# Attention with V as the stationary operand, row sums on VectorE, one-tile FFN passes and DMA transposes, on one core

## The chip, the cores and the metric

The kernel runs on one core of one Trainium2 chip. The metric is the device time of one execution in microseconds (us), and less is better. TensorE does the matmuls, ScalarE (ACT) the exps and tanhs, VectorE (DVE) the elementwise work, GpSimd (POOL) a few small steps of the layer norms, and SyncE (SP) issues every DMA on one queue. Quoted times are medians of several executions. All runs below were timed beside the kernel before on the same chip.

## The reference, cut to what matters

The layer works on 2048 tokens of width 1024: attention with 32 query heads of 32 that share one K and one V head, then a gated FFN of width 3584. Inputs are bf16.

```python
q = (layernorm(x) @ wq)                     # 32 heads x 32; k, v: one head x 32
p = softmax(q @ k.T * 32 ** -0.5)           # 32 x 2048 x 2048 scores
h = x + (p @ v) @ wo
g, u = layernorm(h) @ w_gate, layernorm(h) @ w_up
out = h + (sigmoid(g) * u) @ w_down
```

There are 134 million scores, so 1024 exps of 128 x 1024 each (the profile of the kernel before lists them as 128x1024 x1024, 1052 ns on average), and neither kernel avoids any of them. The rest is matmuls, which TensorE has to run while ScalarE works through the exps.

## The kernel before

Both kernels are written as a plan: a small list scheduler at build time orders the instructions of all engines (`pl.op(engine, function, dependencies, ...)`), and that fixed order is emitted with semaphores. While attention runs, the scheduler puts a visit to the scores (`emit_S`) on TensorE whenever ScalarE is about to run dry, and fills the time between with other groups of matmuls. `Pr` holds exponentiated scores with keys on the partitions. `sigmoid(g)*u` is computed as `0.5*(tanh(g/2)+1)*u`.

A score visit covers 128 queries of 4 heads and 4 key tiles. It has 4 rounds of 4 row-tiled matmuls, because a head of 32 fills only a quarter of the array's rows (the profile lists these matmuls as 32*128 and plain ones as 128*128). Each of the four has its own quarter, and they run side by side: by the median they start 4 ns apart, and the rounds follow each other at about 56 ns, as single plain matmuls of 128 columns do:

```python
for kk in range(KB):                       # KB = 4 key tiles
    for j in range(4):                     # 4 heads, one on each quarter of the rows
        last = pl.op("pe", mm(S_ps[:, bank, kk * P:(kk + 1) * P], kT4[DH * j:DH * (j + 1), kt * P:(kt + 1) * P],
                              QTb[DH * j:DH * (j + 1), c % 2, g, qo:qo + P], True, True, tile_position=(DH * j, 0)), ...)
for i in range(2):                         # two exps, 1024 wide
    exps[u] = pl.op("act", lambda: ACT.activation(out=Pr[:, slot, :]..., in_=S_ps[:, pb:pb + 2, :], func=ACTF.Exp, scale=SCALE), ...)
```

In P V the exponentiated scores are the stationary operand (128 x 128, loaded for each matmul: 8192 loads in the profile for 8192 matmuls), and V with a column of ones moves through (33 columns). The row sum arrives as column 33, so DVE only takes a reciprocal and multiplies. The result has tokens on its partitions, so TensorE transposes it before the output projection:

```python
for j in range(4):
    for kt in range(NT):                   # 16 key tiles
        ... mm(F_ps[:, b, j * VS:j * VS + DH + 1], Pr[:, slot, co:co + P], Vaug[:, kt, 0:DH + 1], kt == 0, kt == NT - 1)
... DVE.reciprocal(rL...); DVE.tensor_tensor(Osb = ov * rL); PE.transpose(Osb -> OT)
```

The FFN works in 8 chunks of 256 tokens. Its gate and up weights stream from HBM once for every chunk, in transfers of 512 KB through a ring:

```python
for w in range(2):                         # gate, up: 256 tokens move
    for dt in range(DT):
        ... mm(F_ps[:, b, w * 256:(w + 1) * 256], wgu[:, sl, w, dt, fo:fo + P], hnT[:, dt, :], dt == 0, dt == DT - 1)
```

The softmax here doesn't subtract the row's maximum and nothing guards it: scores larger than these inputs give would overflow.

## Time and profile before

The first timing gave 1219.02 us (1218.07 to 1223.41, 3 runs). The profiled execution took 1223.8 us.

| | before |
|---|---|
| TensorE busy, 60 to 1060 us | 975.6 of 1000 us |
| ScalarE busy, 60 to 1060 us | 975.4 of 1000 us |
| after the last exp (1060.6 us to the end) | 163 us, almost only FFN matmuls |
| matmuls of P V | 8192, one about every 25 ns |

Here are the page's busy time of each engine (with its share of the span and count of instructions) and its busy tenths in 40 slices of the span:

```profile
PE 1174.0 (96%) x22016; PEld 835.1 (68%) x22016; DVE 316.4 (26%) x838; ACT 1042.1 (85%) x1283; POOL 47.2 (4%) x109
...
PE   4899979999999999999999999999999999999999
...
ACT  6899999999999999999999999999999989711120
```

The last five digits of the ACT row are the tail, in which ScalarE has almost nothing left and TensorE is still full. These are the page's chain of waits by engine, and two of its groups (busy us, mean ns of one, idle time before):

```profile
PE 63%; ACT 31%; issue 3%; DVE 2%; POOL 0%; DMA 0%
...
L495 ACT ACTIVATE Pr<-S_ps 128x1024 bf16<-128x1024 f32 x1024 | 972.4, 1052 | 26.4 <-PE S_ps L330 25.9
...
L330 PE MATMUL F_ps<-Vaug,Pr 128*128 128x33 bf16 x8192 | 244.4, 178 | 2.4 <-issue 1.5
```

The view by windows has, for each stretch, its length and then the busy time of PE, PEld, DVE, ACT and POOL (with counts), the granted TensorE clock, the busy share of the DMA engines and GB/s:

```profile
60.00:1060.00 1000.00, 975.59 (x20038) 686.54 (x20036) 239.31 (x635) 975.40 (x1171) 20.15 (x45) 0.99 0.39 111
...
1060.00:1224.00 164.00, 159.59 (x1283) 117.21 (x1279) 35.97 (x80) 23.14 (x58) 1.34 (x3) 1.00 0.63 163
```

Two engines are full at once for 1000 us. This is how TensorE's time looks in the timeline (start us, length us, and matmuls in a run):

```profile
502.98 0.40 PE L330 MATMUL S_ps<-QTb,kT 32*128 32x128 bf16 x16
503.31 1.52 PE L330 MATMUL F_ps<-Vaug,Pr 128*128 128x33 bf16 x54
504.68 0.27 PE L330 MATMUL F_ps<-hnT,ring 128*128 128x256 bf16 x1
504.88 0.40 PE L330 MATMUL S_ps<-QTb,kT 32*128 32x128 bf16 x16
```

A run of 54 P V matmuls takes 1.52 us with its last latency included.

### The profile page before, as it was taken

The page shows a single profiled execution, that of the slowest core. Times are in us where ns is not written, and L with a number is a line of the kernel's source. Part 1 is how long each engine was busy: PE and PEld are TensorE (multiplying, and loading weights), DVE is VectorE, ACT ScalarE, POOL GpSimd, SP SyncE. Part 2 cuts the span into 40 slices and gives each one's busy share as a digit, 9 for nine tenths or more (in the row PEclk, how much of TensorE's full clock was granted, in tenths as well). Part 3 has the DMA queues.
Part 4 walks back from the last instruction along what each step waited for, and adds up shares of the span by engine and source line. Part 5 has one row for each costly group of instructions (what it writes and reads, how often), then busy time and mean ns, then how long its engine had stood idle before and what let it go on. Part 6 is the DMA issues. An engine that isn't in the chain of part 4 may idle for free.

```text
span 1223.8 us, 47137 instructions
## 1 busy us (share of the span) xinstructions
PE 1174.0 (96%) x22016; PEld 835.1 (68%) x22016; DVE 316.4 (26%) x838; ACT 1042.1 (85%) x1283; POOL 47.2 (4%) x109
## 2 busy tenths in 40 slices
PE   4899979999999999999999999999999999999999
PEld 3665557785678756877568675778657776587684
DVE  8523321212222222223121222132222212232121
ACT  6899999999999999999999999999999989711120
POOL 6100000000000000000000000000000000000000
PEclk9999989999999999999999999999999999999999
DMA  9411175562056601565016460256303653089390
GB/s 320 116 28 41 42 260 156 148 173 64 20 149 174 192 20 46 150 191 148 16 50 191 119 170 20 70 165 184 111 20 86 172 148 102 15 224 263 105 252 18
DMA packets 258612, 151.02 MB, mean 123 GB/s; under 512 B 7280, under 2 KB 248944, under 8 KB 258416
## 3 DMA queue, kind: packets, MB, share of 16 engines
q1 hardware_dynamic: 258416, 148.00, 43.1%
q8 instruction: 173, 2.83, 1.0%
q14 instruction: 23, 0.19, 0.0%
HBM read 140.64 MB, written 7.34 MB: 121 GB/s over the span
## 4 chain that ended last, share of the span: by engine, by line
PE 63%; ACT 31%; issue 3%; DVE 2%; POOL 0%; DMA 0%
PE F_ps L330 54%; ACT Pr L495 28%; PE S_ps L330 9%; ACT tnh L669 1%; ACT zone L313 1%; PE F_ps L619 0%; ACT zone L230 0%; DVE OT L566 0%; DVE st L274 0%; DVE st L276 0%; PE F_ps L558 0%; DMA ring<-in_A_x_dram 0%; POOL dsb L287 0%; DVE hnT L625 0%; DVE ring L307 0%
## 5 line engine op out<-in xcount | busy, mean ns | idle before, releaser
L495 ACT ACTIVATE Pr<-S_ps 128x1024 bf16<-128x1024 f32 x1024 | 972.4, 1052 | 26.4 <-PE S_ps L330 25.9
L330 PE MATMUL F_ps<-hnT,ring 128*128 128x256 bf16 x3584 | 440.6, 275 | 2.5 <-DVE OT L566 1.2
L330 PEld LDWEIGHTS F_ps<-hnT,ring 128*128 128x128 bf16 x3584 | 332.5, 98 | 61.3 <-issue 3.1
L330 PEld LDWEIGHTS F_ps<-Vaug,Pr 128*128 128x128 bf16 x8192 | 229.7, 96 | 28.1 <-issue 4.1
L330 PE MATMUL F_ps<-Vaug,Pr 128*128 128x33 bf16 x8192 | 244.4, 178 | 2.4 <-issue 1.5
L330 PE MATMUL S_ps<-QTb,kT 32*128 32x128 bf16 x8192 | 208.5, 218 | 15.4 <-ACT Pr L495 10.1
L330 PE MATMUL F_ps<-zone,hact 128*128 128x512 bf16 x896 | 213.2, 380 | 0.8 <-DVE OT L566 0.5
L330 PEld LDWEIGHTS S_ps<-QTb,kT 32*128 32x128 bf16 x8192 | 119.2, 93 | 127.9 <-ACT Pr L495 81.6
L676 DVE SCALAR_TENSOR_TENSOR hact<-tnh,F_ps 128x256 bf16<-128x256 f32 x224 | 94.3, 421 | 384.0 <-ACT tnh L669 383.9
L669 ACT ACTIVATE tnh<-F_ps 128x256 f32<-128x256 f32 x224 | 90.7, 405 | 115.0 <-PE F_ps L330 115.0
L330 PEld LDWEIGHTS F_ps<-zone,hact 128*128 128x128 bf16 x896 | 79.2, 98 | 91.3 <-DVE OT L566 0.7
L330 PE MATMUL F_ps<-zone 128*128 128x256 bf16 (+2 forms) x512 | 76.5, 292 | 3.1 <-POOL rstd L290 1.2
L707 DVE SCALAR_TENSOR_TENSOR h_sb<-F_ps,h_sb 128x512 bf16<-128x512 f32 x32 | 22.1, 692 | 203.1 <-PE F_ps L330 203.1
L330 PE MATMUL F_ps<-wo_sb,OT 128*128 128x512 bf16 x256 | 64.2, 381 | 3.8 <-DVE OT L566 3.7
L531 DVE RECIPROCAL rL<-F_ps 128x4 f32<-128x4 f32 x128 | 23.4, 183 | 133.7 <-PE F_ps L330 133.5
L330 PEld LDWEIGHTS F_ps<-zone 128*128 128x128 bf16 x512 | 37.5, 98 | 24.2 <-ACT zone L230 1.4
L284 POOL TENSOR_SCALAR zb<-mvb 128x1 bf16<-128x1 bf16 x32 | 7.5, 233 | 1026.4 <-DVE mvb L280 1026.1
L330 PEld LDWEIGHTS F_ps<-wo_sb,OT 128*128 128x128 bf16 x256 | 21.0, 97 | 28.4 <-DVE OT L566 6.9
L533 DVE TENSOR_TENSOR Osb<-F_ps,rL 128x128 bf16<-128x128 f32 x128 | 37.2, 291 | 3.8
L594 DVE TENSOR_TENSOR h_sb<-F_ps,xres 128x512 bf16<-128x512 f32 x32 | 22.1, 692 | 54.4 <-PE F_ps L330 54.4
L337 PE MATMUL F_ps<-ident,zone 128*128 128x128 bf16 x128 | 11.0, 236 | 17.3 <-POOL dsb L287 9.1
L231 DVE CAST hact<-F_ps 128x512 bf16<-128x512 f32 x24 | 16.6, 692 | 40.2 <-PE F_ps L330 40.2
(39 smaller groups left out, 232.4 us busy)
## 6 DMA issues: line engine op xcount, KB each, us to landing
ring<-in_B_w_gate_dram SPq DMA_DIRECT2D x112, 512.0 KB, 4.1
ring<-in_B_w_up_dram SPq DMA_DIRECT2D x112, 512.0 KB, 5.9
zone<-in_B_w_down_dram SPq DMA_DIRECT2D x4, 1792.0 KB, 15.4
ring<-in_A_x_dram SPq DMA_DIRECT2D x16, 256.0 KB, 7.0
xres<-in_A_x_dram SPq DMA_DIRECT2D x16, 256.0 KB, 2.7
out_dram<-h_sb SPq DMA_DIRECT2D x32, 128.0 KB, 1.7
q_scratch<-hact SPq DMA_DIRECT2D x24, 128.0 KB, 1.8
QTb<-q_scratch SPq DMA_DIRECT2D x6, 512.0 KB, 6.3
```

The costliest lines, as they stand in the source:

```text
L231: lambda: DVE.tensor_copy(out=out_ap, in_=in_ap))
L284: f = pl.op("pool", lambda: POOL.tensor_scalar(out=zb[:, ph, t:t + 1], in0=mvb[:, ph, t, 1:2], scalar1=LN_EPS_BF16, scalar2=None, op0=ALU. ...
L313: xnorm[t] = evac(lambda: ACT.activation(out=dst, in_=src, func=ACTF.Copy, scale=sc), lambda: DVE.tensor_scalar(out=dst, in0=src, scalar1= ...
L330: return lambda: PE.matmul(o, lhsT=l, rhs=r, start=start, stop=stop, **kw)
L337: return [(lambda dt=dt: PE.transpose(out=tp[:, dt * P:(dt + 1) * P], in_=xn[:, t % 2, dt * P:(dt + 1) * P], identity=ident[:, :]), P, []) ...
L495: exps[u] = pl.op("act", lambda slot=slot, pb=pb: ACT.activation(out=Pr[:, slot, :].rearrange("p (a b) -> p a b", a=2), in_=S_ps[:, pb:pb ...
L531: a = pl.op("dve", lambda: DVE.reciprocal(rL[:, k, :].unsqueeze(2), ov[:, :, DH:DH + 1]), [last], prio=0, occ=70, lat=280)
L533: e = pl.op("dve", lambda: DVE.tensor_tensor(out=Osb[:, hh % 2, (g % 4) * P:(g % 4 + 1) * P].rearrange("p (a b) -> p a b", a=4), in0=ov[:, ...
L594: h_ev[(t, dc)] = pl.op("dve", lambda: DVE.tensor_tensor(out=h_sb[:, t % 4, sl], in0=F_ps[:, b, :], in1=xres[:, t % 2, sl], op=ALU.add), [ ...
L669: a = pl.op("act", lambda: ACT.activation(out=tnh[:, k, :], in_=F_ps[:, b, 0:256], func=ACTF.Tanh, scale=0.5), [last, tn_user.get(k)], pri ...
L676: e = pl.op("dve", lambda: DVE.scalar_tensor_tensor(out=hactT[:, ft, :], in0=tnh[:, k, :], scalar=1.0, in1=F_ps[:, b, 256:512], op0=ALU.ad ...
L707: e = pl.op("dve", lambda: DVE.scalar_tensor_tensor(out=h_sb[:, t % 4, sl], in0=F_ps[:, b, :], scalar=0.5, in1=h_sb[:, t % 4, sl], op0=ALU ...
```

## The change

The intent is to take work off TensorE and to shorten the tail. It has these parts:

1. Scores: a visit covers one key tile for 128 queries of 16 heads (a "half"), with 4 row-tiled matmuls of 512 columns in place of 16 of 128. The exps stay 1024 wide.
2. P V: V is the stationary operand (32 columns), four heads' groups sit side by side on quarters of the array's columns (column tiling), and the scores move through 512 wide: 2048 matmuls in place of 8192. The output then has heads on its partitions, as the output projection wants it, so its transposes go.
3. Row sums: DVE adds the 16 key tiles in bf16 (450 adds of 128 x 2048). `sel` matmuls sum over the partitions, and the reciprocals are spread over the partitions through DRAM. The first two halves use ones as a stationary operand instead.
4. FFN: a pass over one tile of 128 tokens as soon as it is there (two if both are). Weight pieces of 256 KB come on a ring whose direction alternates from pass to pass, and their issue is paced at 250 GB/s. More passes read more weights: 656 pieces of 256 KB in place of 224 of 512 KB.
5. The transposes of the FFN's input are done by DMA and not by TensorE.
6. Tanhs are 512 wide: 112 in place of 224.

The diff, cut to its core (... marks cuts):

```diff
         def emit_S(v):
-            for kk in range(KB):
-                for j in range(4):
-                    ...
-                    last = pl.op("pe", mm(S_ps[:, bank, kk * P:(kk + 1) * P], kT4[DH * j:DH * (j + 1), kt * P:(kt + 1) * P],
-                                          QTb[DH * j:DH * (j + 1), c % 2, g, qo:qo + P], True, True,
-                                          tile_position=(DH * j, 0)), ...)
+            for j in range(4):
+                bank = 2 * ((2 * v + j // 2) % NB) + j % 2
+                last = pe_op(mm(S_ps[:, bank, :], kT4[DH * j:DH * (j + 1), kt * P:(kt + 1) * P],
+                                QTb[DH * j:DH * (j + 1), (c // 2) % 2, 4 * hh:4 * hh + 4, (c % 2) * P:(c % 2 + 1) * P],
+                                True, True, tile_position=(DH * j, 0)),
+                             512, "row", deps if j == 0 else [], j == 3)
...
-                        r.append((mm(F_ps[:, b, j * VS:j * VS + DH + 1], Pr[:, slot, co:co + P], Vaug[:, kt, 0:DH + 1],
-                                     kt == 0, kt == NT - 1), DH + 1, []))
+        def mk_PV(hf, part, sums=False):
+            kts = range(8 * part, 8 * part + 8)
+            def atoms(b):
+                return [(mm(F_ps[DH * j:DH * (j + 1), b, :], ones[:, :] if sums else Vt[:, kt, :], slot_of[(hf, kt)][:, j * 512:(j + 1) * 512],
+                            kt == kts[0], kt == kts[-1], tile_position=(0, DH * j)), 512, ...)
+                        for kt in kts for j in range(4)]
...
+        RAW = (0, 1)
+        def make_add(hf, kt):
+            ...
+            add_op[(hf, kt)] = pl.op("dve", lambda: DVE.tensor_tensor(out=a, in0=in0, in1=slot, op=ALU.add), dp, prio=6,
+                                     **t_dve(2048, 1.92))
+        def mk_SUM(hf):
+            ...
+                return [(mm(F_ps[DH * j:DH * (j + 1), b, 0:64], sel[:, bb, :], a[:, j * 512 + bb * 64:j * 512 + (bb + 1) * 64],
+                            bb == 0, bb == 7, tile_position=(0, DH * j)), 64, ...)
+                        for bb in range(8) for j in range(4)]
...
+    PACE_RATE = 250.0
...
+        def load_hT(t):
+            ...
+            hT_ev[t] = hT_last[t] = dma(lambda: SP.dma_start_transpose(hnT[:, :, t % 2, :], hn[:, :]), f"hT{t % 2}", P * D * 2,
+                                        [hnorm[t], gu_last.get(t - 2)] + (extra_rel if t < 2 else []), prio=0)
+        def start_ffn():
+            ...
+            if t + 1 in hT_ev:
+                ts = (t, t + 1)
+            elif t + 1 in hnorm and hnorm[t + 1].end is not None:
+                return
+            else:
+                ts = (t,)
```

## The prediction

> **What bounds the kernel now.** Two stages. Until about 1060 us attention and FFN interleave and ScalarE and TensorE are both full: in the busy-time window 60:1060 ACT is busy 975.4 and PE 975.6 us. The chain of waits alternates between exps (31%) and matmuls (63%). The 1024 exps take 972.4 us by the groups; in the chain 8 take 7.45 us, pitch 0.93. From 1060 (last exp) to 1224 only TensorE works (159.6 of 164 us): an FFN backlog of two 256-token chunks (896 of 3584 gate/up matmuls). So TensorE work sets the time.
>
> **TensorE work, by pitches read in the timeline.** P V: 8192 matmuls with 33 columns, pitch 25 to 28 ns (64 in 1.8 us), about 232 us. 256-wide dense 109.6 ns (428 in 46.9 us), 512-wide 216, 128-wide transposes 57. A visit to the scores is four rounds of 56 ns plus about 85 ns of gap before and 90 after, 0.40 us.[...]
>
> **What the change does there** (counts from the order of instructions; estimates):
> - P V with V stationary, column-tiled: 544 rounds (512 plus 32 of ones) of about 218 ns = 119 us: saves 113.
> - Transposes of O and h (256) gone: saves 15.
> - Scores: 512 visits, one round of 512 instead of four of 128: still 0.40 us.
> - Gate/up 7168 x 128 wide at 56 ns = 401 us (was 393); down 196 (same).
> - Row-sum matmuls and extra mode switches: +20.
> Total about 1195 -> 1085 us.
>
> **ACT.** Still 1024 exps of 1024; tanh 224 x 256 -> 112 x 512 (about 0.50 us pitch, estimate): 10 us less. With no norm passes on ACT and 128-token query pieces, scores can begin near 15 to 20 us and stay fed; before, 21 exps were done by 60 us. I expect 40 or more.
>
> [...]
>
> **DMA** grows from 151 to about 205 MB (656 slab pieces of 256 KB); share stays under 60%.
>
> **Sum.** ACT: 60 + 984 x 0.93 + about 100 tanh x 0.5 + 2% idle = last exp near 1045. After it: 672 gate/up (38), 252 down (28), P V, projection (6), end (4), about 80 us instead of 164. Time 1128 us, 7.5% less; 8 in 10 between 1106 and 1165. Nearly all of the gain is the shorter tail, paid for by P V, plus 10 to 20 us at the start. Chances: faster by over 2% 0.94, same 0.04, slower 0.02.
>
> **What would show it.** Last exp at 1035 to 1060; tail 70 to 95 us; P V rounds near 218 ns per four matmuls;[...] ACT above 95% and PE above 93% in 60:1000; over 35 exps by 60 us; the chain mostly ACT exps until the last exp.
>
> **What would make it wrong.** Column-tiled weight loads that don't hide[...]; P V waiting for adds, so that slots run out and exps stall; slab loads late in the tail or blocked behind DMA transposes; a fixed order that fits the chip's timing badly.

Two terms are estimates. The 218 ns of a P V round is near the 216 ns of a plain matmul of 512 columns in the trace before; that four column tiles take no longer than one was not shown before the run. The 0.50 us of a tanh of 512 columns lies between the 0.26 us of one of 256 and the 0.90 us of an exp of 1024, from start to start in that trace.

## More of the kernel before

A score visit occupies about 0.42 us of TensorE, and nearly half of that is not streaming: the start times show about 96 ns lost at each change between row-tiled and plain matmuls. (A visit starts 205 ns after the last gate/up matmul of 256 columns, by the median, where the next matmul of its own kind starts after 109.)

## The result, and the profile after

The changed kernel takes 1153.64 us (1152.63 to 1155.52, 4 runs). The kernel before took 1221.22 us in the same rounds (1218.07 to 1230.66). The ratio is 0.9437, with a 95% interval of 0.9394 to 0.9481, so 5.6% less time. Here and below a ratio is the mean time of one kernel's runs over that of the other's of the same rounds, so it is not quite the ratio of the medians. The profiled execution took 1150.8 us, at the same mean granted clock as before (0.993).

These lines answer to those of before. Busy time and slices:

```profile
PE 1103.4 (96%) x15112; PEld 750.7 (65%) x15112; DVE 835.2 (73%) x1042; ACT 1035.4 (90%) x1157; POOL 51.6 (4%) x94
...
PE   5999989999999999999999999999999998999899
...
ACT  5999999999999999999999999999999998989300
```

TensorE is again busy for 96% of the span, although it does much less. Its busy share is no good measure here of how near it is to its limit, because the records of matmuls overlap: one of P V lasts 178 ns on average in the kernel before, and the next starts about 25 ns after it. Busy says 96% before and after, while the matmul streaming counted below fills 86% of the span before and 84% after. The chain and the groups:

```profile
PE 78%; ACT 9%; DVE 6%; DMA 5%; issue 2%; POOL 1%; SPq 0%; DVEq 0%
...
L632 ACT ACTIVATE Pr<-S_ps 128x1024 bf16<-128x1024 f32 x1008 | 965.6, 1031 | 29.9 <-PE S_ps L383 20.8
L607 DVE TENSOR_TENSOR acc<-acc,Pr 128x2048 bf16<-128x2048 bf16 x420 | 513.0, 1221 | 108.8 <-ACT Pr L632 98.9
...
L383 PE MATMUL F_ps<-Pr,Vt 128*32 128x512 bf16 x2016 | 131.6, 382 | 2.8 <-ACT Pr L632 2.3
```

The adds take 1221 ns. The chain now runs mostly through matmuls, with 9% of it in ScalarE. The windows:

```profile
200.00:600.00 400.00, 397.76 (x5660) 276.48 (x5660) 308.88 (x355) 394.04 (x439) 13.35 (x18) 1.00 0.64 194
600.00:1000.00 400.00, 384.97 (x5394) 262.38 (x5393) 302.03 (x344) 384.97 (x427) 13.42 (x18) 0.99 0.61 183
...
1073.00:1151.00 78.00, 71.34 (x980) 64.03 (x976) 17.84 (x32) 6.04 (x11) 1.34 (x3) 0.98 0.69 210
```

The last exp starts at 1072.0 us, where it was 1060.6 before, so it comes later and not earlier. The tail shrank from 163 to 78 us. Within the stage both engines share, the second half (600 to 1000 us) is worse than the first, for both engines. The timeline of P V, and a score visit:

```profile
264.98 0.40 PE L383 MATMUL S_ps<-QTb,kT 32*128 32x512 bf16 x4
265.30 1.91 PE L383 MATMUL F_ps<-Pr,Vt 128*32 128x512 bf16 x32
267.15 0.40 PE L383 MATMUL S_ps<-QTb,kT 32*128 32x512 bf16 x4
```

Thirty-two P V matmuls, eight rounds of four column tiles, take 1.91 us with their last latency. From start to start a round takes 216 ns by the median (its four matmuls start 3 ns apart), as long as one plain matmul of 512 columns (216), so the four column tiles run fully side by side. Their weight loads, one for each matmul with records of 96 ns on average, did not lengthen the round.

To see where the 73 us between the two profiled spans went, I summed TensorE's time in both traces from the starts of its matmuls: the streaming of each kind by its usual distance from start to start at full clock, 96 ns for each change between row tiling, column tiling and none, and what is left as waits. What is left also holds the time that half clock costs (below), by an estimate some 8.5 us in each column: half of the 17.1 us that the records show in each trace.

| TensorE's time, us | before | after | change |
|---|---|---|---|
| until the first matmul | 9.1 | 9.8 | +0.7 |
| P V (after: with ones and `sel` matmuls) | 204.8 | 128.1 | -76.7 |
| gate/up | 392.8 | 401.4 | +8.6 |
| down | 193.3 | 196.3 | +3.0 |
| scores | 119.7 | 115.7 | -4.0 |
| output projection | 55.3 | 55.3 | 0 |
| Q, K, V projections | 65.8 | 66.1 | +0.3 |
| transposes | 21.5 | 7.2 | -14.3 |
| all streaming | 1053.2 | 970.0 | -83.2 |
| changes of tiling | 97.5 (1016) | 110.8 (1154) | +13.3 |
| waits and half clock | 60.7 | 57.3 | -3.4 |

With the end after the last matmul (3.3 and 2.9 us), each column gives its span. So the gain is the saved P V and the saved transposes, less more changes of tiling and narrower FFN matmuls. Between 200 and 600 us, streaming and changes together fill about 98.6 of every 100 us after the change: TensorE is full there. Over the whole span, 57 us of waits and half clock were not removed, and more than half of them (32.8 us) fall after 600 us. What TensorE waited for, in the view of waits (us in total, times, longest):

```profile
PE F_ps L383 <- DMA ring<-in_B_w_up_dram: 8.9, 5, 3.2
...
PE F_ps L383 <- DMA Pr<-in_B_w_gate_dram: 3.2, 1, 3.2
...
PE F_ps L383 <- DMA ring<-in_B_w_gate_dram: 1.8, 3, 1.0
```

These are 13.9 us of waits for FFN weights. (One more, of 2.34 us at 1020.6 us before a gate/up matmul, is put down to a VectorE add that this matmul does not read. It may be a late weight too.) One of them, in the timeline:

```profile
951.31 0.39 PE L383 MATMUL S_ps<-QTb,kT 32*128 32x512 bf16 x4
954.90 2.51 PE L383 MATMUL F_ps<-hnT,ring 128*128 128x128 bf16 x22 [3.19 <-DMA ring<-in_B_w_up_dram]
957.34 0.61 PE L383 MATMUL S_ps<-QTb,kT 32*128 32x512 bf16 x4
```

The first score visit took 0.39 us and the one after the wait 0.61. The clock records say 0.5 for 3.4 us, after this wait and after one of 1.70 us:

```profile
885.10 0.72 PE L383 MATMUL F_ps<-hnT,ring 128*128 128x128 bf16 x10 [1.70 <-DMA ring<-in_B_w_up_dram]
...
887.10 2.31 PE L383 MATMUL F_ps<-wo_sb,OT 128*128 128x512 bf16 x5
```

Five matmuls of 512 columns take 2.31 us there, about 427 ns each and not 216. In all, the records show half clock for 17.1 us of this execution, in five pieces of 3.4 us, each of which begins during a wait or within 2 us of its end (waits of 0.89, 1.70, 3.19, 2.34 and 3.21 us, which end at 165.3, 885.1, 954.9, 1022.9 and 1089.7 us). So these waits seem to cost a second time: that is read from these five and from two runs below, r_dma and u_tr, where the waits for weights fall to 3.2 and 5.2 us and the half clock to none and 0.4 us. Their length alone does not decide it: after a wait of 2.02 us at 622 us the records stay at full clock. (The kernel before had 17.1 us of it too, so this is no difference between the two, but it is time that could be had.)

### The profile page after: what moved, and what is told of

It reads as the page before. It is cut to its first block, busy times and chain, and to the rows that moved or that the text cites. A ratio compares the mean times of both kernels' runs of the same rounds, so it can differ in the third digit from the quotient of the medians.

```text
span 1150.8 us, 34683 instructions
## 1 busy us (share of the span) xinstructions
PE 1103.4 (96%) x15112; PEld 750.7 (65%) x15112; DVE 835.2 (73%) x1042; ACT 1035.4 (90%) x1157; POOL 51.6 (4%) x94
## 4 chain that ended last, share of the span: by engine, by line
PE 78%; ACT 9%; DVE 6%; DMA 5%; issue 2%; POOL 1%; SPq 0%; DVEq 0%
PE F_ps L383 66%; PE S_ps L383 12%; ACT Pr L632 8%; DMA ring<-in_B_w_up_dram 3%; DVE acc L607 1%; DMA ring<-in_B_w_gate_dram 1%; ACT tnh L919 1%; DVE st L329 1%; DVE st L327 1%; DVE zone L267 1%; DMA Pr<-in_B_w_gate_dram 1%; DVE zone L366 0%; DVE ring L359 0%; PE F_ps L401 0%; POOL rstd L346 0%
## 5 line engine op out<-in xcount | busy, mean ns | idle before, releaser
L607 DVE TENSOR_TENSOR acc<-acc,Pr 128x2048 bf16<-128x2048 bf16 x420 | 513.0, 1221 | 108.8 <-ACT Pr L632 98.9
L383 PE MATMUL F_ps<-hnT,ring 128*128 128x128 bf16 x6848 | 439.3, 220 | 15.2 <-DMA ring<-in_B_w_up_dram 8.9
L383 PE MATMUL F_ps<-zone,hact 128*128 128x256 bf16 x1792 | 228.0, 273 | 0.8 <-DVE h_sb L962 0.5
L383 PE MATMUL S_ps<-QTb,kT 32*128 32x512 bf16 x2048 | 202.8, 386 | 7.5 <-ACT Pr L632 6.5
L383 PEld LDWEIGHTS F_ps<-zone,hact 128*128 128x128 bf16 x1792 | 163.0, 98 | 48.1 <-issue 28.8
L383 PE MATMUL F_ps<-Pr,Vt 128*32 128x512 bf16 x2016 | 131.6, 382 | 2.8 <-ACT Pr L632 2.3
L383 PEld LDWEIGHTS S_ps<-QTb,kT 32*128 32x128 bf16 x2048 | 51.5, 91 | 117.2 <-ACT Pr L632 47.5
L925 DVE SCALAR_TENSOR_TENSOR hact<-tnh,F_ps 128x512 bf16<-128x512 f32 x112 | 76.5, 683 | 64.6 <-PE F_ps L383 63.6
L919 ACT ACTIVATE tnh<-F_ps 128x512 f32<-128x512 f32 x112 | 67.6, 604 | 56.1 <-PE F_ps L383 55.7
L383 PE MATMUL F_ps<-zone 128*128 128x512 bf16 (+3 forms) x584 | 76.0, 280 | 1.7 <-ACT zone L266 1.4
L962 DVE SCALAR_TENSOR_TENSOR h_sb<-F_ps,h_sb 128x256 bf16<-128x256 f32 x64 | 26.9, 420 | 27.9 <-PE F_ps L383 27.6
L722 DVE TENSOR_TENSOR oun<-F_ps,oun 128x512 f32<-128x512 f32 x32 | 22.0, 688 | 20.5 <-PE F_ps L383 20.5
```

The costliest lines, as they stand in the source:

```text
L383: return lambda: PE.matmul(o, lhsT=l, rhs=r, start=start, stop=stop, **kw)
L607: add_op[(hf, kt)] = pl.op("dve", lambda: DVE.tensor_tensor(out=a, in0=in0, in1=slot, op=ALU.add), dp, prio=6, **t_dve(2048, 1.92))
L722: oun_ev[(hf, 1)] = pl.op("dve", lambda: DVE.tensor_tensor(out=o, in0=F_ps[:, b, :], in1=o, op=ALU.add), [last, oun_ev[(hf, 0)]], prio=0, ...
L919: box["a"] = pl.op("act", lambda: ACT.activation(out=tnh[:, :], in_=F_ps[:, b, :], func=ACTF.Tanh, scale=0.5), [last, box.get("e")], prio= ...
L925: e = pl.op("dve", lambda: DVE.scalar_tensor_tensor(out=ho, in0=shape(tnh[:, :]), scalar=1.0, in1=shape(F_ps[:, b, :]), op0=ALU.add, op1=A ...
L962: e = pl.op("dve", lambda: DVE.scalar_tensor_tensor(out=h_sb[:, t % NHB, sl], in0=F_ps[:, b, 0:DW], scalar=0.5, in1=h_sb[:, t % NHB, sl], ...
```

## The experiments

The theory: ScalarE no longer sets the pace. TensorE does, through its streaming, its changes of tiling, and its waits for late FFN weights. The rival is the prediction's: ScalarE sets the time of the last exp, so work taken off ScalarE would bring the end nearer. A second question was which parts of the change are worth what, and whether a variant is better than both kernels.

The first four runs below cut work out of the changed kernel while keeping its planned order of instructions exactly. Their outputs are wrong, which doesn't matter for the times. The others change the plan, so the scheduler's order moves as well, and a few microseconds of them may be that. A change against the changed kernel is the difference of the two ratios to before, times the before of that run (1220 to 1225 us).

### r_act: less work for ScalarE (wrong result)

```diff
-... ACT.activation(out=tnh[:, :], in_=F_ps[:, b, :], func=ACTF.Tanh, scale=0.5)
+... ACT.activation(out=tnh[:, 0:64], in_=F_ps[:, b, 0:64], func=ACTF.Tanh, scale=0.5)   # tnh set to 0 once
```

> The changed kernel with the tanh of the FFN over 64 of its 512 columns: wrong result on purpose, the order of instructions on all engines the same as in the changed kernel. Takes about 0.37 us from each of 112 tanh, about 41 us of ScalarE work, of which some 37 us lie before the last exp. Theory A (ScalarE bounds the attention stage, as I predicted): last exp 30 to 37 us earlier, time near 1118. Theory B (TensorE bounds it, ScalarE waits for scores): time falls by 0 to 12 us.

Measured: 1156.09 us, ratio 0.9442 (0.9414 to 0.9471), so +0.6 us against the changed kernel, which is nothing. The tanhs' busy time fell from 67.6 to 25.4 us, and ScalarE idled instead. This is its window from 200 to 600 us, where the changed kernel had 394.04 us of ACT and 397.76 of PE:

```profile
200.00:600.00 400.00, 396.11 (x5643) 275.78 (x5647) 308.01 (x353) 380.79 (x438) 13.33 (x18) 1.00 0.65 193
```

ScalarE was not the bound: 42 us less work for it moved nothing. The rival falls. (Weights were a little later in this run: 16.9 us of waits for them and 20.5 us of half clock, against 13.9 and 17.1. By these numbers the relief can have hidden a gain of some 5 us, not more.)

### r_pe: less work for TensorE (wrong result)

```diff
-mm(F_ps[:, b, 0:DW], hv[:, ft, t % 2, :], wd_sb[:, ft, sl], ...)
+mm(F_ps[:, b, 0:DW // 2], hv[:, ft, t % 2, :], wd_sb[:, ft, dq * DW:dq * DW + DW // 2], ...)
```

> The changed kernel with every down-projection matmul 128 instead of 256 columns wide: wrong result on purpose, same order. Takes 1792 x about 53 ns = 95 us from TensorE, some 82 before the last exp and 13 after. Theory A (ScalarE bounds): only the tail shrinks, by 13 to 20 us. Theory B (TensorE bounds): 65 to 90 us less, until ScalarE itself is the bound (its instructions back to back would put the last exp near 995 us), so a time of 1065 to 1090.

Measured: 1127.61 us (1123.53 to 1136.26, 6 runs), ratio 0.9190 (0.9158 to 0.9222), so -30 us. The 1792 down matmuls became half as wide, which takes off about 96 us of streaming (1792 times the difference between 109.6 ns for 256 columns and 56 ns for 128). The direction is right. The size is a third of the relief, and a miss against what was expected. The trace (of the slowest of the six runs) shows where most of the rest went. TensorE's score visits now waited for the exps before them to free their bank, first in the changed kernel and then here:

```profile
PE S_ps L383 <- ACT Pr L632: 6.5, 15, 0.9
```

```profile
PE S_ps L383 <- ACT Pr L632: 42.5, 101, 0.9
```

And the waits for weights, which came no faster than before, grew:

```profile
PE F_ps L383 <- DMA ring<-in_B_w_up_dram: 19.5, 12, 4.1
...
PE F_ps L383 <- DMA Pr<-in_B_w_gate_dram: 5.1, 1, 5.1
```

With two smaller lines these sum to 27.9 us, where the changed kernel had 13.9, and half clock rose from 17.1 to 34.9 us. An estimate: 36 us of waits for exps, 14 of waits for weights and half of 17.8 us of half clock make 59 of the 66 us that are missing.

### r_dma: half the FFN weight bytes (wrong result)

```diff
-view[:, 2 * (q % 2):2 * (q % 2) + 2, :],  W[256 * q:256 * q + 256, ...]
+view[:, 2 * (q % 2):2 * (q % 2) + 1, :],  W[256 * q:256 * q + 128, ...]
```

> The changed kernel with each gate/up slab piece half as large (128 KB instead of 256): wrong result on purpose, same order and same number of transfers. Theory C (late slab pieces cost some 20 us, in 600 to 1090 us, by stopping TensorE and by the lower granted clock after it): time falls by 15 to 28 us and the waits of TensorE for slab transfers vanish. Rival (those waits are slack that another wait would take): under 8 us.

Measured: 1132.66 us, ratio 0.9258 (0.9231 to 0.9285), so -22 us. TensorE's waits for weights fell from 13.9 to 3.2 us, and the half-clock time from 17.1 us to none. An estimate from these two, 10.7 us of waits plus half of 17.1 us, explains 19 of the 22. The window from 600 to 1000 us shows it, with the mean clock at 1.00. The changed kernel had 384.97 for both engines there:

```profile
600.00:1000.00 400.00, 392.09 (x5577) 268.68 (x5583) 309.27 (x353) 395.47 (x441) 13.42 (x18) 1.00 0.39 108
```

Late weights therefore cost about 22 us in all, and mostly late in the kernel.

### r_pe_dma: both of the last two (wrong result)

> Both reliefs at once (down-projection matmuls 128 wide and slab pieces of 128 KB), same order, wrong result on purpose. The down-projection relief alone gave 26 us of 95, the slab relief alone 21. If the late slabs ate the rest of the TensorE relief, both together give more than the sum: 60 to 75 us less than the changed kernel (1080 to 1095), with ScalarE busy over 97% from 200 to 1000 us. If ScalarE was already the wall for the first, the two add up to about 47 us (1105) or less.

The edit is the two above together. Measured: 1101.91 us, ratio 0.8991 (0.8959 to 0.9023), so -54.5 us. That is near the sum of the two single runs (-30 and -22): their gains add up, and it lies between the two cases expected. So early weights did not free the rest of r_pe's relief. TensorE's score visits wait for exps as in r_pe (43.9 us), and the window from 200 to 600 us shows how full ScalarE is:

```profile
200.00:600.00 400.00, 374.65 (x5868) 259.69 (x5871) 317.48 (x364) 398.56 (x454) 13.25 (x18) 1.00 0.41 116
```

TensorE now has 25 us to spare in 400, and ScalarE has 1.4 (from 60 to 1000 us it is busy for 99.3%). So ScalarE is the next wall, a few per cent behind TensorE. In this window 454 ScalarE instructions fit where 439 did, 3% more, and while ScalarE's work stays as it is, no relief of TensorE can bring more than that in this stage.

### u_pv: P V with the scores stationary again

```diff
-mm(F_ps[DH * j:DH * (j + 1), b, :], Vt[:, kt, :], slot_of[(hf, kt)][:, j * 512:(j + 1) * 512], ..., tile_position=(0, DH * j))
+mm(F_ps[:, b, i * DH:(i + 1) * DH], slot_of[(hf, kt)][:, i * P:(i + 1) * P], Vt[:, kt, :], ...)      # i: 16 heads
```

The output comes out in the wrong layout, so the result is wrong. A gate, which holds a P V group back until an earlier output projection is planned, keeps the plan from filling up.

> The changed kernel with P V turned back: P is the stationary operand again (128x128) and V moves, 16 matmuls of 32 columns per key tile instead of one round of four column tiles; the output's layout is then wrong, the amount of work right. By the pitch of 25 ns of the kernel before, 16 x 25 = 400 ns instead of about 216 per key tile and half: 544 x 0.185 = +100 us of TensorE, less some 12 us of mode switches that fall away. Theory B (TensorE's work sets the time): +75 to +95 us, so 1230 to 1250, all of it as a longer tail or later last exp. If instead the tail was shortened by the 128-token FFN passes and not by P V: under +30 us.

Measured: 1222.62 us, ratio 0.9986 (0.9957 to 1.0014), so +67 us against the changed kernel, a little less than expected: the whole gain is gone. TensorE is busy for 983.6 of 1000 us from 60 to 1060, and the last exp comes at 1096.7. Everything else of the change is still there, so without the stationary V there is no gain. The size is in line with the -77 us in the table. It is not a clean measure of it: here the weights were hardly late (3.2 us of waits, no half clock), which gives back part of what the longer P V costs.

### u_ones: row sums by ones on TensorE for all halves

```diff
-RAW = (0, 1)
+RAW = tuple(range(NH))
```

The gate of u_pv is added here too.

> Row sums of all 32 halves by matmuls with ones instead of adds on VectorE (right result): 30 x 16 rounds of about 216 ns more on TensorE (104 us), less 30 groups of 32 small matmuls with their switches (about 15 us); 450 adds (549 us) gone from VectorE. Theory B (TensorE sets the time): +75 to +95 us, 1230 to 1250. Rival (the adds on VectorE hold the P buffers and so the exps): +30 us or less.

Measured: 1231.93 us, correct, ratio 1.0045 (1.0004 to 1.0087), so +74 us. VectorE's busy time fell from 835 to 437 us, and TensorE's rose from 1103 to 1194 us. So 480 more rounds of 216 ns on TensorE (an estimate of 104 us, less the 6.5 us of `sel` matmuls) cost three quarters of their size, and 398 us less on VectorE did not make up for it. Moving the row sums to VectorE was needed for the gain. What took off the last quarter is not shown: weights were less late here as well (4.6 us of waits, 3.6 us of half clock), and VectorE was freed in the same run.

### u_pairs and p14: FFN passes of two tiles

```diff
 def start_ffn():
+    if t < 16 and t + 1 not in hT_ev:     # p14: t < 14
+        return
```

Both are correct. They read each weight for two tiles, so they move fewer bytes, and their gate/up matmuls are 256 wide.

> FFN passes of two 128-token tiles only (256 wide gate/up matmuls as before the change; right result): half as many slab loads, 3584 x 109.6 ns instead of 7168 x 56 = 8 us less TensorE work. If the 128-token passes are what shortened the tail, this gives back 40 us or more (1195). If TensorE work sets the time and slab loads cost 20 us: the tail grows by some 25 us, of which 10 to 15 are idle TensorE (the chain from the row sums to the last transpose has less to hide behind), and the slab waits go: 1130 to 1150.

> As u_pairs, but tiles 14 and 15 in passes of their own (right result): slab waits gone before the tail, and the last chain hidden again behind tile 14. 1120 to 1140; if late slabs are not what costs, 1145 to 1160.

Measured: 1180.59 us for u_pairs, ratio 0.9629 (0.9597 to 0.9661), so +23 us, and 1169.41 us for p14, ratio 0.9541 (0.9507 to 0.9576), so +13 us. Both are misses: I expected them to be faster. The weights are no longer late, but the FFN work comes in larger lots, and TensorE starves between them. This is the stretch from 130 to 200 us, first in the changed kernel and then in p14:

```profile
130.00:200.00 70.00, 63.84 (x856) 38.93 (x856) 58.75 (x65) 68.41 (x78) 2.06 (x3) 0.98 0.76 232
```

```profile
130.00:200.00 70.00, 49.07 (x412) 17.57 (x414) 52.47 (x57) 61.28 (x67) 2.27 (x3) 0.73 0.35 95
```

TensorE is busy 15 us less in these 70 us, and its clock falls to 0.73. Over the whole span the records show 64.9 us of half clock in either run, where the changed kernel had 17.1. Halving the bytes by pairs gives away more than the late weights cost.

### pace_off and pace300: the pace of the weight transfers

```diff
-    PACE_RATE = 250.0
+    PACE_RATE = 100000.0                  # pace300: 300.0
```

> The changed kernel without the pacing that lets each 256 KB slab piece start only 1.05 us after the one before, tied to an exp (right result; the scheduler then orders the other work a little differently). Before each late slab the pieces left at exactly this pace while the DMA engines were busy 0.85. If the pacing made the slabs late: 8 to 20 us less (1134 to 1146). If the DMA engines' own rate did: within 6 us of the changed kernel, or slower, because small transfers then queue behind slabs.

> Pacing at 300 instead of 250 GB/s (right result). If pacing made the slabs late: 6 to 15 us less. If the DMA engines' own rate is the limit: within 5 us.

Measured: pace_off 1164.66 us, ratio 0.9535 (0.9499 to 0.9570), so +12 us. pace300 1144.59 us, ratio 0.9370 (0.9341 to 0.9400), so -8 us. Without a pace, TensorE is kept waiting by a DMA transpose instead:

```profile
PE F_ps L383 <- DMA hnT<-hn: 8.6, 2, 8.0
```

The weights are early then, and a transfer that the critical chain needs comes late. So a pace helps this plan, and 250 GB/s looks somewhat too slow for it. (The intervals of pace300 and of the changed kernel, which begins at 0.9394, just touch, so the 8 us are likely and not sure.)

### u_tr: the FFN's input transposed by TensorE again

```diff
-hT_ev[t] = dma(lambda: SP.dma_start_transpose(hnT[:, :, t % 2, :], hn[:, :]), ...)
+queues["hT"].append(Group("hT", ...))     # 8 PE.transpose into F_ps, one DVE copy to hnT
```

> The changed kernel with the transposes of the FFN input back on TensorE (128 matmuls of 57 ns and their mode's gaps: about 8 us; 16 copies of 0.69 us on VectorE), no DMA transposes (right result). In the changed kernel the one DMA queue stood still for 137 us in front of DMA transposes whose input was not ready. Theory B alone: +5 to +10 us. If those halts were what made slab pieces late: -5 to -20 us.

Measured: 1140.04 us, correct, ratio 0.9338 (0.9308 to 0.9367), so -12 us: the best correct version here, and clearly faster than the changed kernel (0.9394 is the lower end of its interval). TensorE's 128 more matmuls are about 7 us of work, and its waits for weights fell from 13.9 to 5.2 us. Half clock fell from 17.1 to 0.4 us. An estimate: 8.7 us of waits and half of 16.7 us, less the 7, make 10 of the 12 us. From 600 to 1000 us PE is busy for 395.44 us, where it was 384.97:

```profile
600.00:1000.00 400.00, 395.44 (x5617) 273.57 (x5614) 309.09 (x356) 391.37 (x435) 15.52 (x18) 1.00 0.59 181
```

Why are the weights less late? All DMAs of both kernels go through one queue, in the planned order. A transfer that waited for its input held everything behind it: in the stretch of the queue below nothing is issued for 15 us, and then a transpose. These are the queue's own waits (SPq) in the changed kernel for the transposes (L804) and for the store of the row sums (L670), and then those of u_tr:

```profile
SPq L804 <- DVE acc L607: 75.7, 6, 16.3
...
SPq L670 <- DVE r_sb L668: 34.3, 12, 10.3
SPq L804 <- DVE r_sb L668: 32.1, 2, 16.2
SPq L804 <- DVE oun L722: 19.4, 3, 15.5
```

```profile
SPq L982 <- DVE h_sb L975: 112.5, 24, 15.3
SPq L670 <- DVE r_sb L668: 110.0, 13, 17.6
```

The halts at the transposes, with two smaller lines some 138 us, are gone in u_tr. (The issue itself of a transpose took 1.28 us in the changed kernel, the median of 16, where that of a weight piece of 256 KB took 0.37.) But the waits at the row-sum store grew from 34 to 110 us, and those at the output store (L969 before, L982 in u_tr) also grew, from 88 to 114 us. So much of the halting only moved to the next transfer in line, and the sum fell by about 36 us. One stretch of the changed kernel's queue shows a case:

```profile
884.57 4.06 SPq L866 DMA_DIRECT2D ring<-in_B_w_up_dram  x4
903.78 1.27 SPq L804 DMA_TRANSPOSE hnT<-hn  x1
...
914.36 2.40 SPq L866 DMA_DIRECT2D ring<-in_B_w_gate_dram  x4
```

No weights are issued from 888.6 to 914.4 us, and then TensorE waits for them at 921 (0.98 us) and at 951 (3.19 us). In u_tr the same pause runs from 886.9 to 906.6 us, and TensorE does not wait there. The pause is shorter, not gone.

### tr_pace: u_tr with the faster pace

> Both mendings together: transposes of the FFN input on TensorE and pacing at 300 instead of 250 GB/s (right result). Alone they gave 13 and 9 us. If both cure the same late slabs (TensorE still waits 5.2 us for slabs with the first alone), little is left: 0 to 5 us less than the first, 1135 to 1140. If they cure different waits: near 1131.

The edit is the two above together, with 5 rounds. Measured: 1142.74 us, correct, ratio 0.9343 (0.9315 to 0.9371), so -11.5 us. That is no better than u_tr alone (-12) although pace300 alone gave -8, so the two cure the same late weights: with both, the trace lists no wait of TensorE for a DMA and no half clock.

## Why the prediction was right or wrong

The predicted time was 1128 us with a range of 1106 to 1165, against 1153.64 us measured. It said faster by over 2%, which came true, and the time lies within its range, 26 us above the middle. Its cause was right in part, and that the time still fell inside the range is partly luck: it took the wrong engine for the bound, and two errors of its sum partly cancel (below). Point by point:

- P V rounds near 218 ns: measured 216. Right, and u_pv confirms that the gain rests on this part.
- What P V saves: predicted 113 us, measured 77. The term for before was too large (232 us, measured 204.8 at 25 ns), and the term for after, predicted at 119 without the row sums, is 128 with them. The sum of TensorE's work after was close (predicted about 1085 us, measured 970.0 + 110.8 = 1081), but that of before (1195) was 44 us too high.
- VectorE: measured 1221 ns an add and 835.2 us. It stays off the path: VectorE has 6% of the chain, and the waits of TensorE that the view puts down to the adds are 3.9 us in all.
- Tail of 70 to 95 us: measured 78. Right, and it is the shorter tail that shows in the span: 163 - 78 = 85 us, less 11 us by which the last exp comes later.
- Start: 39 exps were begun by 60 us (predicted over 35, before 21). Right. The first exp starts at 18.25 us, where it was 27.26. But the last exp comes later, so the 10 to 20 us forecast for the start do not show in the span.
- ACT above 95% and PE above 93% from 60 to 1000 us: 97.4% and 97.5%. Right, but the kernel before has 97.5% for both, so it tells nothing.
- DMA: 218 MB at a share of 62%, not 205 MB and under 60%. Somewhat off.
- The chain mostly in exps until the last exp: wrong. It is 78% matmuls and 9% ScalarE.
- Last exp between 1035 and 1060, near 1045: wrong, measured 1072.0.

The step that failed is "ACT: 60 + 984 x 0.93 + about 100 tanh x 0.5 + 2% idle = last exp near 1045". It took ScalarE for the bound, with TensorE close behind but able to feed it. The pitch was even too high: exps follow each other at 904 to 921 ns, and at 904 ns 984 of them are about 26 us shorter. The idle share was what failed: from 60 to 1073 us ScalarE waited about 74 us and not 20, so 54 us longer. (This is counted from start to start, beyond 904 ns for an exp and 478 ns for a tanh. The busy view shows only 28 us idle, because one exp's record overlaps the next.) The two together are about the 27 us by which 1045 missed. r_act shows that ScalarE was not the bound (-42 us of its work, no change), and r_pe that TensorE was (-96 us of its work, -30 us), with ScalarE close behind. TensorE was full from 200 to 600 us (98.6%), and after that lost about 22 us to late weights and the half clock that followed them (r_dma). The prediction had named late slabs "in the tail or blocked behind DMA transposes" as a risk, but put no term for them in its sum. With those 22 us in the sum, the time would have come out near 1150. That is an estimate, and it leaves other errors of the sum that cancel.

Left open: how much of u_tr's 12 us is due to the queue's shorter halts, and how much to the order that the scheduler replanned, since the two could not be changed apart. It is also open what ends the waits that remain outside the late weights, and how many of the 1154 changes of tiling (111 us) a better order could save. No run here tested that.

## What to carry to other kernels

When two engines are both busy for 97% of a stage, cut work out of each one in turn with the order kept: the one whose relief moves the time is the bound, and the other may be a wall only a few per cent behind it (here 96 us off TensorE bought 30). Sum TensorE's time from start to start, with the changes of tiling (here 96 ns each, 110.8 us for 1154 after the change) and the waits as terms of their own, and not from its busy share (here 96% before and after). On one DMA queue that keeps its order, as here, a transfer that had to wait for its input held every prefetch behind it (some 138 us in front of the transposes), so give such a transfer another way (here that took off 12 us), or count its wait as a cost of the prefetches.
